# W' of batches 1 to 3 by seven block products instead of eight, with stored sums of w_in's blocks and the softmax's division ahead of its transpose

## The chip, the cores and the metric

The kernel runs on one NeuronCore of a Trainium2 chip. The metric is the device time of one execution in microseconds (us). A profile of one such execution gives for each engine which instruction ran when: PE is the matrix engine, with its weight loads (PEld) listed apart, DVE the vector engine, ACT the scalar engine, POOL (GpSimd) and SP mainly issue transfers (DMA) here.

## The reference: channel attention, then an ELU feed-forward layer

```python
qn = q / (norm(q, axis=1) + 1e-6)            # q, k, v: 4 batches x 6080 tokens x 256 channels
kn = k / (norm(k, axis=1) + 1e-6)
s  = kn.transpose(0, 2, 1) @ qn / tau        # 256 x 256 for each batch
a  = exp(s - max(s)); a /= a.sum(-1) + 1e-9
x  = v @ a                                   # 24320 x 256 over all batches
h  = x @ w_in                                # w_in: 256 x 2048
g  = where(h > 0, h, exp(min(h, 0)) - 1)
out = g @ w_out                              # w_out: 2048 x 256
```

## The kernel before

Per batch the kernel makes one matrix W' = a @ w_in (256 x 2048) and then h = v @ W', so the product v @ a is never made. All matrix products are in fp32r: each operand is split into a high and a low part (ACT casts the high part, DVE subtracts it for the low one), and three matmuls (high by high, high by low, low by high) stand for one product.

The 24320 tokens are 48 chunks of 512 or 496 columns, 12 in a batch. The first four chunks go through a first stage whose order is written by hand, up to about 240 us in the trace. From then on the chunks go in 22 pairs, and h of a pair is made as block products: W' and v are each cut into 2 x 2 blocks, and seven products of sums of blocks (Winograd's form) give what eight products of blocks would. `plan_half` lays down one eighth of a pair: seven products into PSUM banks `bank_a`, `bank_b`, `bank_e` (line 1355; `seed` and `keep` on ACT and `up` and `last` on DVE move partial sums between them), then for four results Relu and Exp on ACT (1383, 1386), the ELU's maximum on DVE (1389), the split of g (ACT 1392, DVE 1395), and the products with w_out into `po` (1413 to 1415).

W' of batch 0 is made in the first stage. For batches 1 to 3 these steps are mixed into the pairs of the batch ahead:

- `plan_rows`: rows of q and k are loaded (SP), split and squared (ACT 1519, 1528; DVE 1531, 1534), and their Gram matrix is summed in the one PSUM bank `pe` (PE 1550, matmuls of 256 columns).
- `plan_soft`: norms, softmax (DVE and ACT, one 128-row half `ct` after the other), `total` (`over_sums`: one over the sums of the softmax), the transposes into `pe` (1676) and the split of the transposed matrix into `aT` (ACT 1683, DVE 1687).
- `plan_s`, once for each quarter `fq` of W' (512 of its 2048 columns): POOL loads the split quarter of w_in, 1 MB, from DRAM (`wi_scr`, line 1429), PE makes two groups of 12 matmuls in all (1451 to 1453, each 128x512, one half of W's rows in a group), both in bank `pe`; ACT copies each group out, times one over the sums (1456). Then four block sums on DVE (836), the high parts by a casting DMA that POOL issues (1471), the low parts on DVE (1478): these are the left factors of the seven products of `plan_half`.

Nothing of this runs in program order. `op(engine, cost, due, fn, deps, takes, uses, lands)` records a step with an assumed cost and a due time; `Ring`s hold the buffers that steps take and give back (`row_ring`: two 8 KB slots for raw rows, v and w_in; `w_ring`: two 4 KB slots; `gram_ring`: the one bank `pe`; `acc_ring` and `square_ring`: one slot each). `best_plan` simulates the five engines, always taking the step that is due first among those that can begin first, shifts due times at random in some stretches of 40 us (`CHANCES` holds the seeds), and the kernel is then written in that order. So each engine works through a fixed list, and an instruction that has to wait holds up all that stands behind it on its engine. `SLACK` stretches the assumed costs, `PACE` spaces the due times.

The core of the step that changes, as it is before:

```python
for jt in range(KT):
    whi, wlo = (in_turns(wi.tile[:, y, jt, :]) for y in range(2))
    nc.tensor.matmul(pw, aT[:, 0, jt, cs], whi, start=(jt == 0), stop=False)
    nc.tensor.matmul(pw, aT[:, 0, jt, cs], wlo, start=False, stop=False)
    nc.tensor.matmul(pw, aT[:, 1, jt, cs], whi, start=False, stop=(jt == KT - 1))
```

Of the kernel before, what the change touches and what calls it, by code (L numbers as in the profile page):

```python
# [57 lines left out]
def channel_attention_then_elu_ffn(ctx: ExitStack, tc, q, k, vT, tau, w_in, w_out, outT):  # L58
# [570 lines left out]
    nc.sync.dma_start(w_scr, wf[0])  # L629
# [280 lines left out]
    SLACK = {ACT: 1.005, DVE: 1.005, POOL: 1.0, PE: 1.003, SP: 1.0}  # L910
# [120 lines left out]
    def best_plan():  # L1031
# [28 lines left out]
    PACE = (10.15, 10.15, 10.15, 10.15)  # L1060
# [275 lines left out]
    DUE = {"products": -20.0, "seed": -20.0, "keep": -19.0, "up": -18.0, "last": -15.0, "terms": -8.0, "soft": -92.0, "soft step": 0.0}  # L1336
# [84 lines left out]

    def plan_s(b, fq, t, deps, state_of):


        wi, xs = Buf(row_ring), [Buf(w_ring) for _ in range(2)]

        def load():
            wi.tile = work.tile([P, 2, KT, CH], F32R, tag="qk", bufs=3, name=f"wi_{fq}")
            nc.gpsimd.dma_start(wi.tile, wi_scr[fq])
# [4 lines left out]
        scaled = []  # L1434
# [4 lines left out]
        else:  # L1439
            got = op(POOL, 0.6, t - 20, load, deps[0:1], [wi], lands=3.8)  # L1440
            got.ready = t - 20
        for ct in range(KT if b else 0):
            bank = Buf(gram_ring)

            def items(ct=ct, bank=bank):
                pw = bank.slot()
                cs = slice(ct * P, ct * P + P)
                aT = state_of["aT"]
                for jt in range(KT):
                    whi, wlo = (in_turns(wi.tile[:, y, jt, :]) for y in range(2))  # L1450
                    nc.tensor.matmul(pw, aT[:, 0, jt, cs], whi, start=(jt == 0), stop=False)
                    nc.tensor.matmul(pw, aT[:, 0, jt, cs], wlo, start=False, stop=False)  # L1452
                    nc.tensor.matmul(pw, aT[:, 1, jt, cs], whi, start=False, stop=(jt == KT - 1))  # L1453

            def scale(ct=ct, bank=bank):
                nc.scalar.activation(
                    x_items(2 * ct, 2 * ct + 2), halves_of_turns(bank.slot()), AF.Copy, scale=state_of["rs"][:, ct : ct + 1]
                )
# [26 lines left out]
    def plan_rows(b, state_of):  # L1485
# [14 lines left out]
        for g in range(begun, NG):  # L1500
            t = t0 + PACE[b - 1] * (1 + over * (g - begun) / (NG - begun))
# [61 lines left out]
    def plan_soft(b):  # L1563
# [105 lines left out]
        total = op(DVE, 0.35, later(), lambda: over_sums(s["rs"]), exps)  # L1669
# [93 lines left out]
```

## Time and profile before

| | |
|---|---|
| median of 3 runs | 2062.77 us (2062.23 to 2062.91) |
| the profiled execution's own time | 2062.74 us |
| its span, first to last instruction | 2061.0 us |
| PE busy | 2053.7 us (100%) |
| ACT busy | 1717.3 us (83%) |
| DVE busy | 1671.0 us (81%) |
| POOL busy | 60.6 us (3%) |
| mean granted clock of PE | 0.999 of full speed |

A matmul's record is longer than the time for which it holds PE, because the next one starts before it ends: the distance between two starts is the price of one in a stream. A record of DVE or ACT likewise ends somewhat after the next one's start can lie. The span leaves out about 1.7 us of the execution's own time.

### The profile page before, as it was taken

Reading aid. Unit: us, or ns where it says so; the run is one execution under the profiler, and the core shown is the slowest. Engines: PE = TensorE matmul, PEld = TensorE weight load, DVE = VectorE, ACT = ScalarE, POOL = GpSimd, SP = SyncE. Lnnn points to the kernel's source line nnn. Section 1 sums busy time; section 2 is a strip of 40 time slices with the busy share of each in tenths; the row PEclk is TensorE's granted clock in tenths of the full one; section 3 lists DMA queues with packets and bytes.
Section 4 is the critical chain, followed back from the end, with each engine's and each line's share of the span. In section 5 each row is a group of like instructions: output and inputs, shape, how many; then the busy total and the mean of one; then the engine's idle time right before and its main releaser. Section 6 shows DMA issues by size and latency. Waiting matters only on the chain.

```text
span 2061.0 us, 28279 instructions
## 1 busy us (share of the span) xinstructions
PE 2053.7 (100%) x9976; PEld 1813.2 (88%) x9976; DVE 1671.0 (81%) x2597; ACT 1717.3 (83%) x3120; POOL 60.6 (3%) x118
## 2 busy tenths in 40 slices
PE   9999999999999999999999999999999999999998
PEld 8888888899888888889888888888888888888887
DVE  7988989888888888887888878878889777677765
ACT  6888789888788988888888888888887788788776
POOL 0000000000100000000000000000001000000000
PEclk9999999999999999999999999999999999999999
DMA  9343332112322121221322212212123110110000
GB/s 357 132 151 99 106 108 82 66 59 96 113 97 82 47 87 57 72 64 46 109 92 89 89 46 75 72 54 84 55 79 135 41 57 16 41 56 16 21 31 20
DMA packets 71806, 164.95 MB, mean 80 GB/s; under 512 B 7536, under 2 KB 16752, under 8 KB 69616
## 3 DMA queue, kind: packets, MB, share of 16 engines
q1 hardware_dynamic: 55968, 118.53, 16.8%
q0 software_dynamic: 15408, 44.11, 6.6%
q8 instruction: 78, 1.28, 0.3%
q14 instruction: 64, 0.52, 0.1%
q10 hardware_dynamic: 288, 0.51, 0.1%
HBM read 100.40 MB, written 31.20 MB: 64 GB/s over the span
## 4 chain that ended last, share of the span: by engine, by line
PE 99%; ACT 0%; DMA 0%; issue 0%; DVE 0%; ACTq 0%; SPq 0%
PE bank_b L1355 16%; PE po L1413 14%; PE po L1414 14%; PE po L1415 14%; PE bank_e L1355 11%; PE bank_a L1355 11%; PE pe L1550 4%; PE gram L497 2%; PE po L423 1%; PE po L422 1%; PE po L421 1%; PE ph L383 1%; PE ph L382 1%; PE ph L381 1%; PE pe L1453 1%; PE pe L1452 1%
## 5 line engine op out<-in xcount | busy, mean ns | idle before, releaser
L1413 PE MATMUL po<-g,wo 128*128 128x512 f32 (+1 forms) x938 | 353.7, 377 | 0.0
L1415 PE MATMUL po<-g,wo 128*128 128x512 f32 (+1 forms) x938 | 353.3, 377 | 0.0
L1414 PE MATMUL po<-g,wo 128*128 128x512 f32 (+1 forms) x938 | 353.2, 377 | 0.0
L1386 ACT ACTIVATE more_e<-more_e 128x512 f32<-128x512 f32 (+1 forms) x562 | 344.2, 632 | 2.5
L1395 DVE TENSOR_TENSOR g<-more_e,g 128x512 fp32r<-128x512 f32 (+1 forms) x371 | 251.2, 681 | 45.4 <-ACT g L1392 43.8
L1392 ACT CAST g<-more_e 128x512 fp32r<-128x512 f32 (+1 forms) x371 | 227.2, 618 | 35.5 <-PE po L1414 18.3
L1389 DVE SCALAR_TENSOR_TENSOR more_e<-more_e,bank_b 128x512 f32<-128x512 f32 (+1 forms) x141 | 96.0, 681 | 141.3 <-ACT more_e L1386 141.3
L1415 PEld LDWEIGHTS po<-g,wo 128*128 128x128 f32 x938 | 177.3, 189 | 22.9
L1413 PEld LDWEIGHTS po<-g,wo 128*128 128x128 f32 x938 | 177.4, 189 | 22.1 <-ACT o_both L1144 0.4
L1414 PEld LDWEIGHTS po<-g,wo 128*128 128x128 f32 x938 | 177.4, 189 | 21.4
L1383 ACT ACTIVATE more_e<-bank_b 128x512 f32<-128x512 f32 (+1 forms) x141 | 83.7, 593 | 128.8 <-PE bank_b L1355 126.4
L1413 PE MATMUL po<-wp,wo 128*128 128x512 f32 (+1 forms) x470 | 177.3, 377 | 0.0
L1415 PE MATMUL po<-wp,wo 128*128 128x512 f32 (+1 forms) x470 | 177.0, 377 | 0.0
L1414 PE MATMUL po<-wp,wo 128*128 128x512 f32 (+1 forms) x470 | 177.0, 377 | 0.0
L1395 DVE TENSOR_TENSOR wp<-more_e,wp 128x512 fp32r<-128x512 f32 (+1 forms) x191 | 130.0, 681 | 22.1 <-ACT wp L1392 21.3
L1355 PE MATMUL bank_a<-term,wp 128*128 128x512 f32 (+1 forms) x528 | 141.5, 377 | 0.0
L1364 DVE TENSOR_TENSOR bank_e<-bank_b,e 128x512 f32<-128x512 f32 (+1 forms) x176 | 121.4, 690 | 22.7 <-ACT e L1362 19.3
L1392 ACT CAST wp<-more_e 128x512 fp32r<-128x512 f32 (+1 forms) x191 | 117.5, 616 | 18.6 <-DVE more_e L1389 9.6
L1368 DVE TENSOR_TENSOR e<-bank_b,e 128x512 f32<-128x512 f32 (+1 forms) x176 | 119.9, 681 | 8.8 <-PE bank_b L1355 8.0
L1550 PEld LDWEIGHTS pe<-rows 128*128 128x128 f32 x804 | 108.7, 191 | 6.2
L1389 DVE SCALAR_TENSOR_TENSOR more_e<-more_e,bank_a 128x512 f32<-128x512 f32 (+1 forms) x141 | 95.4, 676 | 19.8 <-ACT more_e L1386 19.1
L1355 PEld LDWEIGHTS bank_a<-term,wp 128*128 128x128 f32 x528 | 99.3, 189 | 13.0
(325 smaller groups left out, 4755.9 us busy)
## 6 DMA issues: line engine op xcount, KB each, us to landing
v<-in_v_dram SPq DMA_DIRECT2D x13, 1024.0 KB, 4.9
out_dram<-o_both SPq DMA_DIRECT2D x48, 256.0 KB, 2.0
wi<-wi_scr POOLq DMA_DIRECT2D x12, 1024.0 KB, 5.1
w<-in_q_dram SPq DMA_DIRECT2D x34, 256.0 KB, 2.7
w<-in_k_dram SPq DMA_DIRECT2D x34, 256.0 KB, 2.9
v<-in_v_dram SPq DMA_DIRECT2D x8, 992.0 KB, 4.9
more<-in_q_dram SPq DMA_DIRECT2D x30, 256.0 KB, 2.6
more<-in_k_dram SPq DMA_DIRECT2D x30, 256.0 KB, 2.9
```

What stands on the lines that cost most here:

```text
L1355: nc.tensor.matmul(into, ws[x], y, start=(begin and k == 0), stop=(k == 2), skip_group_check=True)
L1364: up = op(DVE, 0.605 * share, t + DUE["up"], lambda: nc.vector.tensor_add(ve, vb, p7.slot[:, 0:n]), [m6, keep], uses=[bank_b, bank_e, p7])
L1368: last = op(DVE, 0.605 * share, t + DUE["last"], lambda: nc.vector.tensor_add(vp(), vb, vp()), [m5, up], uses=[bank_b, p7])
L1383: nc.scalar.activation(ev(), h(), AF.Relu, scale=-1.0)
L1386: nc.scalar.activation(ev(), ev(), AF.Exp, scale=-1.0)
L1389: nc.vector.scalar_tensor_tensor(ev(), ev(), -1.0, h(), op0=ALU.add, op1=ALU.max)
L1392: nc.scalar.copy(g_part(g, 0, n), halves(ev()))
L1395: nc.vector.tensor_sub(g_part(g, 1, n), halves(ev()), g_part(g, 0, n).bitcast(F32))
L1413: nc.tensor.matmul(o, wo[:, f, 0, ds], hi, start=begin, stop=False)
L1414: nc.tensor.matmul(o, wo[:, f, 1, ds], hi, start=False, stop=False)
L1415: nc.tensor.matmul(o, wo[:, f, 0, ds], lo, start=False, stop=end)
L1550: nc.tensor.matmul(pg, r.tile[:, kx, 1, z, cs], in_turns(r.tile[:, qx, 0, z, :]), start=(g == begun and ct == 0 and z == 0 and m == 0), st ...
```

## The change

It touches batches 1 to 3 and the stores that serve them.

- **W' by seven products.** `plan_w` takes the place of the 12 matmuls of 512 columns in `plan_s`: the transposed softmax matrix and each quarter of w_in are cut into 2 x 2 blocks (128 x 128 and 128 x 256), and seven products of 3 matmuls of 256 columns each are made in two takes of bank `pe`. Three partial sums are copied out by ACT (`keep` twice, `c11`), five additions on DVE (`u`, `v`, `c22` and two outputs) finish the four blocks of W'.
- **Sums of w_in's blocks, stored once.** `plan_sums` (in batch 0, once per quarter) loads the exact quarter from `w_scr`, makes the four sums T1 to T4 on DVE, splits them (ACT, DVE) and stores them in `t_scr`. So `w_scr` now holds all four quarters, and `put_by` stores a split quarter of w_in as four blocks. `plan_w` loads a quarter in two takes of `row_ring` (three blocks, then four), four DMAs on POOL, 1.75 MB, where `plan_s` had one of 1 MB.
- **The softmax.** `over_sum` divides its rows by their sums ahead of the transposes, so that W' comes out without a scale. The transposed matrix is kept exact (`a_exact`), DVE makes four block sums of 128 x 128, and eight blocks are split instead of four. The low parts take `square_ring`'s slot, so the next batch's squares wait for it until W' is done.
- **Numbers of the plan.** Assumed costs of ACT and DVE times 1.0075 instead of 1.005, `PACE` 10.22 instead of 10.15, the softmax due 98 us ahead of its batch instead of 92, the rows of q and k spread over 35 paces from pace 2.2 on instead of 36.5, quarters of W' due earlier or later by `W_AT`, other seeds in `CHANCES`.

```diff
+    t_scr = dram.tile([FQ, P, 2, 4, CH // 2], F32, name="t_scr")
+    wi_scr = dram.tile([FQ, 2, 2, P, KT, CH // 2], F32, name="wi_scr")
+    def put_by(fq, parts):
+        for x in range(2):
+            for h in range(2):
+                nc.sync.dma_start(wi_scr[fq, x, h], parts[:, x, :, h * CH // 2 : (h + 1) * CH // 2].bitcast(F32))
...
     def split_wf(fq):
         wis[fq] = work.tile([P, 2, KT, CH], F32R, tag="qk", bufs=3, name=f"wi_0_{fq}")
-        split(wis[fq][:, 0], wis[fq][:, 1], wf.pop(fq))
-        nc.sync.dma_start(wi_scr[fq], wis[fq].bitcast(F32))
+        exact = wf.pop(fq)
+        split(wis[fq][:, 0], wis[fq][:, 1], exact)
+        put_by(fq, wis[fq])
+        nc.sync.dma_start(w_scr[fq], exact)
...
-    SLACK = {ACT: 1.005, DVE: 1.005, POOL: 1.0, PE: 1.003, SP: 1.0}
+    SLACK = {ACT: 1.0075, DVE: 1.0075, POOL: 1.0, PE: 1.003, SP: 1.0}
...
-    PACE = (10.15, 10.15, 10.15, 10.15)
+    PACE = (10.22, 10.22, 10.22, 10.22)
...
+    def plan_sums(fq, t):
+        exact, sums, parts = Buf(w_ring), Buf(w_ring), Buf(row_ring)
...
+        x = op(SP, 0.1, t, lambda: nc.sync.dma_start(exact.slot(), w_scr[fq]), (), [exact], lands=1.9)
+        for y, name in enumerate(("T1", "T3", "T2", "T4")):
+            x = op(DVE, 0.35, t + 8 + y, lambda name=name: total(name, block), [x], [] if y else [sums], [exact, sums] if y else [exact])
+        x = op(ACT, 0.945, t + 14, hi, [x], [parts], [sums])
+        x = op(DVE, 1.145, t + 17, lo, [x], uses=[parts, sums])
+        return op(SP, 0.1, t + 20, lambda: nc.sync.dma_start(t_scr[fq], parts.tile.bitcast(F32)), [x], uses=[parts], lands=3.8)
+
+    def plan_w(fq, t, deps, s, xs, item):
...
+        for k in range(2):
+            for y in sources[k]:
+                due = t - W_LOAD + W_NEXT * k
+                x = op(POOL, 0.6, due, lambda k=k, y=y: load(k, *y), [*deps[0:1], t_done[fq]], [blocks[k]], lands=0.95 * (y[1] - y[0]))
...
+                for n, (i, j) in enumerate(((0, 0), (0, 1), (1, 0))):
+                    nc.tensor.matmul(
+                        at_bank(k, half),
+                        s["aT"][i][:, z],
+                        in_turns(blocks[of].tile[:, j, y]),
...
+        m1 = product(0, 0, "A11", "B11", True, t)
+        p1 = keep(0, 0, 4, t + 1, [m1])
+        m6 = product(0, 1, "S2", "T2", False, t + 0.5, [m1])
+        u = add(lambda: item(5), lambda: at_bank(0, 1), lambda: item(4), t + 2, [m6, p1], banks[0:1])
+        m2 = product(0, 0, "A12", "B21", False, t + 1.5, [p1])
+        c11 = op(ACT, 0.3, t + 3, lambda: nc.scalar.copy(halves(item(0)), halves_of_turns(at_bank(0, 0))), [m2], xs[0:1], banks[0:1])
+        m5 = product(1, 0, "S1", "T1", True, t + 3)
+        m7 = product(1, 1, "S3", "T3", False, t + 3.5, [m5])
+        p7 = keep(1, 1, 6, t + 4, [m7])
...
+        m4 = product(1, 1, "A22", "T4", False, t + 4.5, [p7])
+        m3 = product(1, 0, "S4", "B22", False, t + 5.5, [c22])
...
-            z = op(PE, 1.3, t - 10 + 3 * ct, items, [got, *deps], [bank], [wi, state_of["aT_buf"]], turn=t - 10 + ct)
-            scaled.append(op(ACT, 0.6, t - 8 + 3 * ct, scale, [z], xs[0:1], [bank]))
+            scaled = plan_w(fq, t, deps, state_of, xs, lambda y: x_items(y, y + 1)[:, 0])
...
+        for ct in range(KT):
+            x = op(DVE, 0.25, later(), lambda ct=ct: over_sum(ct), [x])
...
+        x = e = op(ACT, 0.465, later(), a_exact, [pt], (), [turns])
+        for k in range(4):
+            x = op(DVE, 0.21, later(), lambda k=k: a_sum(k), [x])
+        high = op(ACT, 0.51, later(), lambda: a_hi(0), [e, parts, pn], s["aT_bufs"])
```

What stands in a row on PE where batch 2's first quarter of W' is made. The names: `wi` the loaded w_in, `aT` the split softmax matrix (`aT_acc` its high, `aT_sq` its low part), `scr_r` and `wp` left factors, `po` the sums of the output. Before:

```order
L1451 MATMUL pe<-wi_8155,aT_8424 128x512
L1452 MATMUL pe<-wi_8155,aT_8424 128x512
L1453 MATMUL pe<-wi_8155,aT_8424 128x512
L1413 MATMUL po_466<-g_2029,wo 128x496
L1414 MATMUL po_466<-g_2029,wo 128x496
L1415 MATMUL po_466<-g_2029,wo 128x496
L1355 MATMUL bank_b<-terms,scr_r 128x496 x3
```

The same place in the changed kernel, PE:

```order
L1488 MATMUL pe<-wi_0_8313,aT_acc_8572 128x256 x2
L1488 MATMUL pe<-wi_0_8313,aT_sq_8573 128x256
L1362 MATMUL bank_b<-term_1687,scr_r 128x496 x3
L1488 MATMUL pe<-wi_0_8313,aT_acc_8572 128x256 x2
L1488 MATMUL pe<-wi_0_8313,aT_sq_8573 128x256
L1362 MATMUL bank_e<-term_2696,wp_381 128x496 x3
L1362 MATMUL bank_a<-terms_too,wp_381 128x496 x3
L1488 MATMUL pe<-wi_1_8341,aT_acc_8572 128x256 x2
L1488 MATMUL pe<-wi_1_8341,aT_sq_8573 128x256
```

A quarter that was two runs of six full-width matmuls is now seven runs of three half-width ones; between the first product of a bank (m1, just ahead of these rows' first run, m6) and the product that waits for its copy (m2, the second run here) stands one other product of three matmuls.

POOL's list from the first load of batch 2's w_in on, before (`terms` and `term` are v's blocks of a coming pair, `scr_r` and `wp` the left factors):

```order
L1429 DMA wi_8155<-wi_scr 128x2048
L1313 DMA terms<-v_8006 128x496
L1429 DMA wi_8227<-wi_scr 128x2048
L1429 DMA wi_8475<-wi_scr 128x2048
L1471 DMA wp_380<-w_1993 128x768
```

POOL's list at the same place in the changed kernel:

```order
L1467 DMA wi_0_8313<-t_scr 128x2x256
L1467 DMA wi_0_8313<-wi_scr 128x2x512
L1467 DMA wi_1_8341<-wi_scr 128x2x256
L1467 DMA wi_1_8341<-t_scr 128x2x768
L1467 DMA wi_0_8626<-t_scr 128x2x256
L1467 DMA wi_0_8626<-wi_scr 128x2x512
L1467 DMA wi_1_8666<-wi_scr 128x2x256
L1467 DMA wi_1_8666<-t_scr 128x2x768
L1565 DMA scr_r<-w_2009 128x1024
```

Where two quarters of w_in had a slot each, one quarter now fills both slots, and the loads of the next one (`wi_0_8626`) stand behind the last product that reads `wi_0_8313`.

DVE's list around the split of batch 1's transposed softmax matrix, before:

```order
L283 TENSOR_SCALAR sums<-sums 128x2
L284 RECIPROCAL sums<-sums 128x2
L1395 TENSOR_TENSOR g_1966<-more_e,g_1966 128x496
L1364 TENSOR_TENSOR bank_e<-bank_b,e_1886 128x496
L1687 TENSOR_TENSOR aT_4392<-pe,aT_4392 128x512
```

DVE's list there in the changed kernel:

```order
L1766 TENSOR_SCALAR a_671<-a_671,sums 128x256 x2
L1402 TENSOR_TENSOR wp_382<-more_e,wp_382 128x2x248
L1375 TENSOR_TENSOR e_1902<-bank_b,e_1902 128x496
L1396 SCALAR_TENSOR_TENSOR more_e<-more_e,e_1901 128x496
L1792 TENSOR_TENSOR aT_sums_4334<-aT_4333 128x128
L1396 SCALAR_TENSOR_TENSOR e_1903<-e_1903,bank_a 128x496
L1792 TENSOR_TENSOR aT_sums_4334<-aT_sums_4334,aT_4333 128x128
L1803 TENSOR_TENSOR aT_sq_4341<-aT_4333,aT_acc_4340 128x512
```

The division (the first row) now stands ahead of the transposes, and sums of blocks and a second split (further down) come behind them.

## Rows read from the trace of the kernel before

**Rows 1.** The page's head, its busy times by engine, and the first line of the chain of work that ended last (shares of the span).

```profile
span 2061.0 us, 28279 instructions
PE 2053.7 (100%) x9976; PEld 1813.2 (88%) x9976; DVE 1671.0 (81%) x2597; ACT 1717.3 (83%) x3120; POOL 60.6 (3%) x118
...
PE 99%; ACT 0%; DMA 0%; issue 0%; DVE 0%; ACTq 0%; SPq 0%
```

**Rows 2.** The timeline of PE at the four widest openings between two starts behind the first stage: start in us, record's length, line, tiles, form, count; in brackets the idle time that the profile counts.

```profile
241.24 0.38 PE L1415 MATMUL po<-g,wo 128*128 128x512 f32 x1
241.66 0.92 PE L1355 MATMUL bank_e<-term,scr_r 128*128 128x512 f32 x3
...
271.46 0.38 PE L1415 MATMUL po<-g,wo 128*128 128x512 f32 x1
272.19 0.91 PE L1355 MATMUL bank_b<-terms,s_later 128*128 128x512 f32 x3 [0.35 <-ACT bank_b L1360]
272.94 0.81 PE L1355 MATMUL bank_a<-terms,wp 128*128 128x512 f32 x3
...
275.36 0.38 PE L1415 MATMUL po<-g,wo 128*128 128x512 f32 x1
275.70 0.92 PE L1355 MATMUL bank_e<-term,s_later 128*128 128x512 f32 x3
...
284.00 0.38 PE L1415 MATMUL po<-g,wo 128*128 128x512 f32 x1
284.36 0.91 PE L1355 MATMUL bank_b<-terms,s_later 128*128 128x512 f32 x3
```

**Rows 3.** Who waited for whom on PE behind the first stage: us in total, times, longest.

```profile
PE bank_b L1355 <- ACT bank_b L1360: 0.3, 1, 0.3
```

**Rows 4.** The timeline of PE where batch 1's first quarter of W' is made, columns as in rows 2.

```profile
520.03 0.38 PE L1451 MATMUL pe<-wi,aT 128*128 128x512 f32 x1
...
521.11 0.38 PE L1453 MATMUL pe<-wi,aT 128*128 128x512 f32 x1
521.33 0.79 PE L1355 MATMUL bank_e<-term,wp 128*128 128x496 f32 x3
521.96 0.79 PE L1355 MATMUL bank_b<-terms,scr_r 128*128 128x496 f32 x3
...
523.66 0.38 PE L1453 MATMUL pe<-wi,aT 128*128 128x512 f32 x1
```

**Rows 5.** The timeline of PE in a stretch with matmuls of 256 columns beside ones of 512, same columns.

```profile
705.54 0.83 PE L1550 MATMUL pe<-rows 128*128 128x256 f32 x6
706.21 0.81 PE L1355 MATMUL bank_e<-terms,s_later 128*128 128x512 f32 x3
706.86 0.81 PE L1355 MATMUL bank_b<-terms_too,s_later 128*128 128x512 f32 x3
```

**Rows 6.** A group of PE's instructions by line and form over the span, one of three alike (lines 1451, 1452, 1453): count, busy us, mean ns of one record, idle before.

```profile
L1451 PE MATMUL pe<-wi,aT 128*128 128x512 f32 x48 | 18.2, 379 | 0.0
```

**Rows 7.** Groups of DVE's and of ACT's instructions by line and form, from 240 us on: count, busy us, mean ns of one, idle before.

```profile
L1531 DVE TENSOR_TENSOR acc<-acc,sq 128x1024 f32<-128x1024 f32 x65 | 79.5, 1222 | 9.3 <-ACT sq L1528 8.8
...
L1653 DVE TENSOR_SCALAR a<-a,rk 128x256 f32<-128x256 f32 x6 | 2.1, 348 | 0.0
L1687 DVE TENSOR_TENSOR aT<-pe,aT 128x512 fp32r<-128x512 f32 x3 | 2.1, 690 | 0.2 <-ACT aT L1683 0.2
...
L1600 DVE TENSOR_TENSOR a<-pe,a 128x256 f32<-128x256 f32 x2 | 0.7, 416 | 0.0
...
L1631 DVE TENSOR_SCALAR rk<-ry,itau 128x4 f32<-128x4 f32 x3 | 0.7, 219 | 0.0
...
L1519 ACT CAST rows<-w 128x1024 fp32r<-128x1024 f32 x35 | 36.9, 1053 | 1.2 <-DMA w<-in_k_dram 0.5 <-DVE terms_too L1317 0.3 <-PE pe L1550 0.3
...
L1604 ACT COPY a<-pe 128x256 f32<-128x256 f32 x4 | 1.4, 389 | 0.0
```

**Rows 8.** Busy time of each engine (PE, PEld, DVE, ACT, POOL, with counts), granted clock, DMA share and GB/s in four stretches.

```profile
240.00:460.00 220.00, 219.62 (x1111) 193.65 (x1110) 193.07 (x285) 194.70 (x346) 4.75 (x9) 1.00 0.25 84
300.00:350.00 50.00, 50.00 (x253) 44.05 (x252) 46.97 (x68) 47.19 (x85) 1.58 (x3) 1.00 0.30 101
460.00:600.00 140.00, 140.00 (x687) 125.41 (x687) 117.31 (x207) 115.07 (x221) 9.47 (x18) 1.00 0.30 102
...
1450.00:1600.00 150.00, 150.00 (x732) 134.23 (x732) 127.77 (x222) 123.45 (x238) 10.01 (x19) 1.00 0.27 93
```

**Rows 9.** The timeline of ACT at the first copy of W' out of its bank: start, length, and the idle time that the group of rows 4 that ended last had caused.

```profile
521.53 0.69 ACT L1456 ACTIVATE more<-pe,sums 128x512 f32<-128x512 f32 x1 [0.60 <-PE pe L1453]
```

**Rows 10.** POOL's transfers: the issue of w_in's load (line 1429), min/median/max ns; its time from issue to landing, min/median/max us; the same for the casts of the left factors (line 1471); one load in the timeline of POOL.

```profile
L1429 POOL DMA_DIRECT2D wi<-wi_scr x12: 527/527/530, 485.3 to 1567.3; - x12
...
DMA to landing us min/median/max: 4.9/5.1/7.1
...
DMA to landing us min/median/max: 2.8/3.4/7.3
...
524.34 0.53 POOL L1429 DMA_DIRECT2D wi<-wi_scr  x1 [30.19 <-PE pe L1453]
```

**Rows 11.** The timeline of PE in the first stage, matmuls of 256 columns whose operands are plain f32.

```profile
51.82 2.76 PE L497 MATMUL pe<-scr 128*128 128x256 f32 x12
54.41 1.89 PE L324 MATMUL pw<-wf,aT 128*128 128x256 f32 x8
```

More of the change, by code (lines that the diff above doesn't have):

```diff
@@ L1335, in channel_attention_then_elu_ffn @@
     }
-    DUE = {"products": -20.0, "seed": -20.0, "keep": -19.0, "up": -18.0, "last": -15.0, "terms": -8.0, "soft": -92.0, "soft step": 0.0}
+    DUE = {"products": -20.0, "seed": -20.0, "keep": -19.0, "up": -18.0, "last": -15.0, "terms": -8.0, "soft": -98.0, "soft step": 0.0}
     def plan_half(p, fq, j, t, terms, s_done, outs):
@@ L1422, in plan_s, with flat @@
+    def flat(x):
+        return x.rearrange("p a (b t) -> p (a b) t", b=2)
+    A_BLOCKS = ("A11", "A21", "A12", "A22", "S1", "S2", "S3", "S4")
+    SUM_BLOCKS = ("T1", "T3", "T4", "T2")
+    PACKS = (("B11", "B21", "T2"), ("T1", "T3", "T4", "B22"))
+    t_done = {}
     def plan_s(b, fq, t, deps, state_of):
[L1425 to L1429, printed above, removed]
+        xs = [Buf(w_ring) for _ in range(2)]
@@ L1439, in plan_s @@
         else:
[L1440 to L1458, printed above, removed]
-            z = op(PE, 1.3, t - 10 + 3 * ct, items, [got, *deps], [bank], [wi, state_of["aT_buf"]], turn=t - 10 + ct)
-            scaled.append(op(ACT, 0.6, t - 8 + 3 * ct, scale, [z], xs[0:1], [bank]))
+            scaled = plan_w(fq, t, deps, state_of, xs, lambda y: x_items(y, y + 1)[:, 0])
         y = None
@@ L1500, in plan_rows @@
         for g in range(begun, NG):
-            t = t0 + PACE[b - 1] * (1 + over * (g - begun) / (NG - begun))
+            t = t0 + PACE[b - 1] * (ROWS_FROM + over * (g - begun) / (NG - begun))
             n = min(2, RP - 2 * g)
@@ L1676, in transposes @@
                     nc.tensor.transpose(pt[:, jt, ct * P : ct * P + P], s["a"][:, ct, jt * P : jt * P + P], ident)
-        pt = op(PE, 0.4, later(), transposes, exps, [turns], turn=t + 1)
-        s["aT_buf"] = Buf(acc_ring)
-        def aT_hi():
-            s["aT"] = work.tile([P, 2, KT, C], F32R, tag="acc", bufs=1, name=f"aT_{b}")
-            nc.scalar.copy(s["aT"][:, 0], turns.slot().rearrange("p (k c) -> p k c", k=KT))
-        def aT_lo():
-            aT = s["aT"]
-            nc.vector.tensor_sub(aT[:, 1], turns.slot().rearrange("p (k c) -> p k c", k=KT), aT[:, 0].bitcast(F32))
@@ L1689, in plan_soft, with blocks, a_exact @@
-        x = op(ACT, 0.51, later(), aT_hi, [pt, parts], [s["aT_buf"]], [turns])
-        x = op(DVE, 0.605, later(), aT_lo, [x], uses=[turns, s["aT_buf"]])
-        return [last, x, total], s
+        pt = op(PE, 0.4, later(), transposes, [x], [turns], turn=t + 1)
+        s["aT_bufs"] = [Buf(acc_ring), Buf(square_ring)]
+        def blocks(lo, hi):
+            return s["exact"][lo // 4].rearrange("p k (c x) -> p (k c) x", c=2)[:, lo % 4 : lo % 4 + hi - lo]
+        def a_exact():
+            s["exact"] = [work.tile([P, KT, C], F32, tag="a", bufs=1, name=f"aT_{b}")]
+            s["exact"] += [tiny.tile([P, KT, C], F32, tag="early", bufs=1, name=f"aT_sums_{b}")]
+            nc.scalar.copy(s["exact"][0], turns.slot().rearrange("p (k c) -> p k c", k=KT))
@@ new lines, in a_sum, with a_hi @@
+        def a_sum(k):
+            a11, a21, a12, a22, s1, s2, s3, s4 = (blocks(y, y + 1) for y in range(8))
+            to, one, other = ((s1, a21, a22), (s2, s1, a11), (s3, a11, a21), (s4, a12, s2))[k]
+            (nc.vector.tensor_sub if k else nc.vector.tensor_add)(to, one, other)
+        def a_hi(k):
+            if k == 0:
+                s["aT"] = [
+                    work.tile([P, 8, P], F32R, tag=tag, bufs=1, name=f"aT_{tag}_{b}") for tag in ("acc", "sq")
+                ]
+            nc.scalar.copy(s["aT"][0][:, 4 * k : 4 * k + 4], blocks(4 * k, 4 * k + 4))
@@ L1693, in channel_attention_then_elu_ffn @@
+        high = op(ACT, 0.51, later(), lambda: a_hi(1), [x, high], uses=s["aT_bufs"])
+        low = op(DVE, 0.605, later(), lambda: a_lo(1), [high, low], uses=s["aT_bufs"])
+        return [last, low], s
     s_ring = {fq: Ring(fq) for fq in range(FQ)}
@@ L1710, in channel_attention_then_elu_ffn @@
                 s_done[0, fq] = plan_s(0, fq, PACE[0] * (2 * fq - FIRST_S), (), None)
+            for fq in range(FQ):
+                t_done[fq] = plan_sums(fq, SUMS_AT + SUMS_STEP * fq)
         else:
```

96 lines of the change are left out of this document (81 added, 15 removed).

## The prediction

> **What bounds the kernel now.** I began with the head of the page and the chain that ended last [rows 1]: PE is busy for 2053.7 of 2061.0 us, and 99% of the chain is PE. ACT and DVE work for 83% and 81% of the span, but the chain does not pass through them. A busy PE could still hide waits inside overlapping records, so I read the distances between starts next. Behind the first stage the four widest openings [rows 2] are 271.46 to 272.19 us (0.73, where one matmul of 512 columns takes 0.216 [rows 5]: 0.51 lost), 241.24 to 241.66 (0.20 lost), 284.00 to 284.36 (0.14) and 275.36 to 275.70 (0.12). The group of three behind such an opening takes 0.75 (272.19 to 272.94) where 0.65 is usual, 0.1 more each time. Together 1.4 us; and the list of waits on PE has a single line there, 0.3 us [rows 3]. So the time is the length of PE's list. A change gains what it takes out of that list and loses what it makes PE wait, and work on the other engines counts only through such a wait.
>
> **PE's list: the gain.** A quarter of W' is 12 matmuls of 512 columns; six start between 520.03 and 521.33 [rows 4], 0.2158 each with the finer 0.65/3 of [rows 5] beside it (0.2167). With three lines of 48 [rows 6] there are 144: 144 x 0.2158 = 31.07 us. The changed kernel has 12 quarters of 7 x 3 = 21 matmuls of 256 columns, 252. Six of that width take 0.67 us (705.54 to 706.21 [rows 5]), 0.1117 each: half a wide one would be 0.1079, so halving costs 0.004 each. 252 x 0.1117 = 28.14 us. The list gets shorter by **2.9 us**, against the 3.9 us that one product in eight would be without that surcharge. Both forms are fp32r with one weight load each, and weight loads ran beside the matmuls in either. The transposes, Gram matrices and the products of the pairs keep their counts.
>
> The Trainium skill, "TensorE: Matmul & The Clock Gate", section Back-to-back issue gap, gives N/2.4 + 2.5 ns for N columns, that is 109 ns at 256 and 216 at 512, and by that the gain would be 3.6 us; this trace agrees at 512 and not at 256 (112).
>
> **DVE and ACT: more work, under cover.** A quarter adds five additions of 128x256, read from PSUM or SBUF, at 0.416 (line 1600 [rows 7]): 2.1 us, so 8.3 us a batch. The softmax adds two row scalings at 0.348 (line 1653), a second split at 0.690 (line 1687), and four sums of 128x128, a form that the trace lacks: between 0.219 (128x4, line 1631) and 0.416 (128x256), and I take 0.32, half way, as the width is half way too: 0.70 + 0.69 + 1.28 = 2.7 us. So 11.0 us of DVE a batch. From 460 to 600 us DVE works 117.3 of 140 us [rows 8]; 128.3 would be 92%. At batch 3 (1450 to 1600) 127.8 of 150 becomes 138.8, 93%. In batch 0, `plan_sums` adds four times 4 x 0.416 + 1.222 (line 1531's width) = 2.9, 11.6 us in all, to a stretch (240 to 460 us) with 193.1 of 220: 93%. That such shares can be borne is shown by 300 to 350 us: DVE 46.97 and ACT 47.19 of 50 (94%), and PE 50.00. ACT loses two copies of 0.69 [rows 9] a quarter and gains three of 0.389 (line 1604), 0.2 less; the sums' casts add four times 1.05 (line 1519) once. I take nothing for either engine; the bound above is a rival below.
>
> **New waits inside W'.** Products m2 and m4 reuse a half bank that ACT has just copied. A copy began 0.42 us after the last matmul of its group had begun (521.11 [rows 4] to 521.53 [rows 9]) and takes 0.389, so m2 may start 0.81 us behind m1's last start. At the tightest place (batch 2's first quarter) m6 and one product of 496 columns stand between: 0.11 + 0.34 + 0.63 (521.33 to 521.96 [rows 4]) = 1.08 us. That holds if ACT is free; behind a step like the 0.69 of [rows 9] it is late by up to 0.4. Twice in 12 quarters that is 0 to 10 us; nearest is the same shape in the pairs, `seed` behind m1, 176 times in this run with 0.3 us of wait in all [rows 3]. I take 0.
>
> **POOL: the reload.** Four loads a quarter for one: 36 more issues of 0.53 us [rows 10], on an engine 3% busy. Queued behind them on POOL are the casts of v's blocks and of the left factors, whose order the plan has moved with them. But the cover shrinks. Before, each quarter had one slot: the third was loaded at 524.34, when the first was through, and the second, already there, lay between. Now a quarter fills both slots of `row_ring`, and the next quarter's first take is loaded only when the last product of the present first take is through. In PE's new list 24 matmuls of 496 columns (0.209) and 12 of 256 stand between these two: 5.02 + 1.34 = **6.4 us**, at five places (7.0 at a sixth); elsewhere it is over 10 us. What has to fit: a load was issued 0.68 us after the start of the matmul that freed its slot (523.66 [rows 4] to 524.34 [rows 10]), 0.47 behind that matmul's place; the second issue 0.53 later; landing, for pairs of 512 and 384 KB issued in this way, 2.8 to 7.3 us, median 3.4 (line 1471 in [rows 10]; now it is 512 and 256 KB). Together 4.4 us, with 2.0 to spare; at the maximum 8.3, 1.9 late. I take 0 and keep six times 0 to 1.9 for the range.
>
> A rule of the Trainium skill speaks against these loads: "SBUF — State Buffer", section SBUF: two separate sides, says that a DMA issued from POOL has its descriptors written through a port that VectorE can hold for a whole instruction, so that the transfer starves meanwhile. Estimated from one DVE step of 0.69 us ahead of each of two issues that is 1.4 us, 5.8 in place of 4.4, still below 6.4; no row shows it, as all 12 issues took 527 to 530 ns with DVE at 84%.
>
> **SP and the softmax's chain.** SP gets 23 more issues in the whole run; the blocks' stores stand ahead of q and k rows that are squared four steps later, and SP mostly waits. Nothing. The longer softmax chain (2.7 us of DVE, a copy and a cast on ACT) is due 6 us earlier, and after W' its left factors are still read some 40 us later in PE's list, as before. Nothing.
>
> **The sum.** The profiled execution took 2062.74 us, the median of the runs is 2062.77; from the latter 2062.77 - 2.93 = **2059.8 us**, 0.14% less. What a measurement of this kernel can tell from no change is about 0.2%, 4.1 us: faster ends at 2058.6, slower begins at 2066.9.
>
> **The rivals.**
> 1. *The openings close too.* The order behind 236 us is planned anew with slower assumed engines, and 1.4 us of openings [rows 2] could go: 2059.8 - 1.4 = 2058.4, just over the line to faster. For it: they lie at the start of the planned part. Against: DVE gets more work exactly there.
> 2. *Some reloads come late.* Two of six at the maximum landing: 2059.8 + 3.8 = 2063.6. For it: 2.0 us to spare and landings up to 7.3. Against: the median.
> 3. *DVE becomes the bound in batch 0 (slower).* The 11.6 us of `plan_sums` fall into 240 to 460 us. If they land where DVE is full, each of them delays splits that PE needs: 2059.8 + 11.6 = 2071.4. It decides where DVE's demand passes the stretch: 193.1 + 11.6 leaves 15 of 220 us; an added 7.1 us of wait is needed to be slower by over 0.2%. All six reloads late (2059.8 + 11.4 = 2071.2) is the same side by another door.
> 4. *A narrow matmul costs more than half.* From 31.07/252 = 0.123 us on, the list gets longer. The f32 ones of the same width took 0.216 (51.82 to 54.41, 12 of them [rows 11]); at that price 252 x 0.216 = 54.4, 23 us more: 2086. Then the change would not do what it says. Against: its tiles are fp32r as in the 0.1117 of [rows 5]. The same section of the skill gives sustained spacings of about 131 ns at 512 and 81 at 128, by which narrowing is a loss as well; the trace has 216 at 512 and contradicts it.
>
> **How the numbers follow.** Forecast 0.64, rival 1 0.14, rival 2 0.10, rival 3 with its second door 0.10, rival 4 0.02. Faster is rival 1, 0.14; same the forecast and rival 2, 0.74; slower rivals 3 and 4, 0.12. For 8 in 10 the range leaves out rivals 3 and 4 (0.12) and half of rival 1 (0.07): from 2058.2 to 2064.0, which holds two late reloads, or 4 of the 10 us of waits inside W'.
>
> **What would show it.** Right: a group of three matmuls of W' takes 0.335 us from start to start; PE's openings sum to about what they did; DVE at 91 to 94% in the stretches named and PE at 100% there. Wrong: lines in PE's waits that name `pe` and a load of `wi` (rival 2), or ACT's or DVE's copies and sums of `pe` (the chain in W'); openings between 290 and 460 us behind DVE (rival 3); the narrow matmuls at another spacing (rival 4).

## The result, and the profile after

The changed kernel takes **2073.31 us** (median of 4 runs, 2072.46 to 2074.42) against 2062.5 of the kernel before beside it: 10.8 us more, ratio 1.0051, 95% interval 1.0039 to 1.0063. The forecast of 2059.8 and its whole range (2058.2 to 2064.0) were wrong; by the prediction's own bound of 0.2% this is slower, an outcome to which it gave 0.12. The profiled execution took 2072.46 us, its span is 2070.7.

Head of the page, busy time by engine and the chain by engine, as in [rows 1]:

```profile
span 2070.7 us, 28454 instructions
...
PE 2055.9 (99%) x10084; PEld 1811.0 (87%) x10084; DVE 1704.9 (82%) x2698; ACT 1727.9 (83%) x3142; POOL 88.7 (4%) x154
...
PE 95%; DVE 2%; ACT 1%; DMA 1%; issue 0%; SPq 0%; POOL 0%; ACTq 0%; DVEq 0%
```

PE's part of the chain was 99%; now DVE and ACT stand in it. PE's waits (in all, times, longest), which had a single line behind the first stage [rows 3]:

```profile
PE bank_b L1362 <- ACT bank_b L1367: 3.1, 2, 2.5
PE pe L1488 <- DVE more L1504: 1.4, 5, 0.4
...
PE pe L1644 <- DVE rows L1628: 0.9, 1, 0.9
PE bank_e L1362 <- DVE more_e L1396: 0.7, 3, 0.3
PE bank_b L1362 <- DVE bank_e L1371: 0.5, 1, 0.5
PE pe L1488 <- DMA wi<-wi_scr: 0.4, 2, 0.2
```

Line 1488 is a product of W', 1362 a product of a pair, 1644 the Gram matrix. The windows of [rows 8] again (PE, PEld, DVE, ACT, POOL, clock, DMA share, GB/s):

```profile
240.00:460.00 220.00, 217.76 (x1105) 191.52 (x1104) 198.45 (x297) 193.92 (x337) 4.74 (x9) 1.00 0.34 112
300.00:350.00 50.00, 48.39 (x243) 41.65 (x242) 46.22 (x68) 45.33 (x80) 1.57 (x3) 1.00 0.39 132
460.00:600.00 140.00, 137.15 (x702) 122.25 (x701) 121.85 (x227) 114.75 (x228) 17.73 (x28) 1.00 0.37 113
1450.00:1600.00 150.00, 148.75 (x756) 132.45 (x755) 123.75 (x223) 119.64 (x231) 16.28 (x26) 1.00 0.30 92
```

PE stood for 2.2, 1.6, 2.9 and 1.3 us in them, and in the second and the fourth it waits although DVE and ACT are both *less* busy than before (DVE 46.97 and 127.77, ACT 47.19 and 123.45).

For a full account I took the distance of every two starts on PE behind 235 us, less the median distance for that pair of widths, and added up the differences over 15 ns. I call these **openings** (a slower matmul behind a stand is counted with them):

| kernel | median us | openings us | of it at products of W' |
|---|---|---|---|
| before | 2062.5 | 6.3 | 0 |
| changed | 2073.3 | 19.6 | 5.6 |

Openings grew by 13.3 us. PE's last matmul ended at 2055.27 us before and at 2065.57 after, so the list without openings went from 2049.0 to 2046.0: 3.1 us shorter. Of these, 0.2 us belong to the first stage, which came to its first product of a pair at 229.57 us instead of 229.80; the planned part is 2.8 us shorter. 13.3 - 3.1 = 10.2 us, against 10.3 between the two ends. Three places hold most of it: products of W' (5.6 us, at 13 places), batch 0 from 250 to 332 us (4.4, where the kernel before has 1.5 by the same count from 235 to 335), and a single opening at 501 us (2.65).

A place in W' (timeline of the changed kernel: start, length, engine, line; the shown instructions only):

```profile
561.87 0.37 ACT L1501 COPY w<-pe 128x256 f32<-128x256 f32 x1
...
562.63 0.37 PE L1422 MATMUL po<-g,wo 128*128 128x496 f32 x1
562.67 0.42 DVE L1504 TENSOR_TENSOR w<-pe,w 128x256 f32<-128x256 f32 x1
...
563.14 0.30 PEld L1488 LDWEIGHTS pe<-wi,aT_acc 128*128 128x128 f32 x2 [0.52 <-DVE w L1504]
563.14 0.49 PE L1488 MATMUL pe<-wi,aT_acc 128*128 128x256 f32 x2
```

The product at 563.14 is m2. It writes the half of `pe` that ACT had copied out from 561.87 to 562.24; yet it starts 0.05 us after DVE has read the *other* half (the sum `u`, 562.67 to 563.09). PE's list of this program says the same. These are the rows of the first quarter of batch 1 (m1, m6 and m2, first matmul of each), with the waits that the program holds:

```
1916 L1488 MATMUL pe<-wi_0_4120,aT_acc_4340 128x256 [waits DMASW1_49]
1919 L1488 MATMUL pe<-wi_0_4120,aT_acc_4340 128x256 [waits DMASW0_49,Activation_49]
1926 L1488 MATMUL pe<-wi_0_4120,aT_acc_4340 128x256 [waits DVE_49]
```

m6 waits for ACT (the copy p1 of m1's half) and m2 for DVE (u), though `plan_w` gives the planner m1 alone for m6 and p1 alone for m2. The Trainium skill, "PSUM — Partial Sum Buffer", section PSUM bank collisions raise a hardware error, states a rule that such a wait follows: accesses of two engines are to be guarded by bank, not by address. The trace agrees (m2 starts 0.05 us behind the end of u), and the prediction did not weigh it.

### The profile page after: what moved, and what is told of

Its sections match the earlier page's. It is cut to its first block, busy times and chain, and to the rows that moved or that the text cites. A ratio compares the mean times of both kernels' runs of the same rounds, so it can differ in the third digit from the quotient of the medians.

```text
span 2070.7 us, 28454 instructions
## 1 busy us (share of the span) xinstructions
PE 2055.9 (99%) x10084; PEld 1811.0 (87%) x10084; DVE 1704.9 (82%) x2698; ACT 1727.9 (83%) x3142; POOL 88.7 (4%) x154
## 3 DMA queue, kind: packets, MB, share of 16 engines
q1 hardware_dynamic: 61328, 126.39, 17.9%
## 4 chain that ended last, share of the span: by engine, by line
PE 95%; DVE 2%; ACT 1%; DMA 1%; issue 0%; SPq 0%; POOL 0%; ACTq 0%; DVEq 0%
PE bank_b L1362 16%; PE po L1420 14%; PE po L1422 14%; PE po L1421 14%; PE bank_e L1362 11%; PE bank_a L1362 11%; PE pe L1644 4%; PE gram L503 2%; PE pe L1488 1%; PE po L429 1%; PE po L427 1%; PE po L428 1%; PE ph L387 1%; PE ph L389 1%; PE ph L388 1%; DMA wi<-wi_scr 1%
## 5 line engine op out<-in xcount | busy, mean ns | idle before, releaser
L1362 PE MATMUL bank_e<-term,wp 128*128 128x512 f32 (+1 forms) x528 | 141.5, 377 | 0.0
L1362 PE MATMUL bank_a<-term,wp 128*128 128x512 f32 (+1 forms) x432 | 115.7, 377 | 0.0
L1644 PE MATMUL pe<-rows 128*128 128x256 f32 x804 | 110.7, 275 | 0.9 <-DVE rows L1628 0.9
```

The costliest lines, as they stand in the source:

```text
L1362: nc.tensor.matmul(into, ws[x], y, start=(begin and k == 0), stop=(k == 2), skip_group_check=True)
L1644: nc.tensor.matmul(pg, r.tile[:, kx, 1, z, cs], in_turns(r.tile[:, qx, 0, z, :]), start=(g == begun and ct == 0 and z == 0 and m == 0), st ...
```

## The experiments

**Theory 1:** the waits between the halves of `pe`, unknown to the planner, make the openings of W'. **Theory 2:** the DVE work of `plan_sums` makes those of batch 0 (the prediction's rival 3). **Theory 3:** the order that comes out of the new numbers makes what lies outside W', whatever the amount of work. The rivals stand with each run. The kernel before, run beside these kernels each time, took 2062.4 to 2063.2 us.

### u_off and readers_off: no DVE read of the other half

```diff
-u = add(..., lambda: at_bank(0, 1), lambda: item(4), ...)
+u = add(..., lambda: item(4), lambda: item(4), ...)
 # readers_off, besides:
-c22 = add(..., lambda: halves_of_turns(at_bank(1, 0)), lambda: halves_of_turns(item(7)), ...)
+c22 = add(..., lambda: halves_of_turns(item(7)), lambda: halves_of_turns(item(7)), ...)
```

> The changed kernel with one DVE step altered: u, the sum of the copied product m1 and of m6, no longer reads m6 from bank pe (it adds the copy to itself, so W' is not the reference's). Orders, instruction counts and durations stay. Theory 1 (halves of one bank): m2, which needs only the half that ACT copied out, in fact waits until DVE has read the other half. Then the openings of the changed kernel that end with a DVE sum of pe (those before 563.14, 587.71, 1073.01, 1100.13, 1580.88 and 1593.16 us) vanish, 2.0 us with the slower group behind each, and the time is about 2071.3. Rival (the prediction's own term: ACT's copy p1 comes late): m2 still waits for the copy, the openings stay within 0.1 us each and the time stays at 2073.3.

> As the run before, and c22 too reads no bank (W' is not the reference's). Theory 1 (halves of one bank, with DVE's sums as the late step): the openings at 1029.55, 1053.66, 1536.87, 1561.88 and 1585.04 go as well, 2.7 us, and with them the two that follow 2 to 3 us later at 1032.5 and 1539.9 (0.9): with the 2.0 of u some 5.6 us in all, about 2067.7. Of the openings ahead of products of W' only the one at 575.35 stays, which ends with a load. Rival (ACT's copies p1 and p7 come late): the openings move by under 0.1 us each, and the time stays within 1 us of 2073.3. Second rival (a wait only goes to the next step): the openings go but others of the same size stand behind them in the pairs, and the time falls by less than half of 5.6 us.

Measured: u_off 2073.42 us (2070.82 to 2074.95), span 2069.0, openings 17.9, at W' 4.3. readers_off 2070.63 (2068.66 to 2070.73), span 2068.9, openings 17.5, at W' 2.2. The same place in u_off (timeline of PE):

```profile
562.68 0.37 PE L1422 MATMUL po<-g,wo 128*128 128x496 f32 x1
562.89 0.38 PE L1488 MATMUL pe<-wi,aT_acc 128*128 128x256 f32 x2
563.11 0.28 PE L1488 MATMUL pe<-wi,aT_sq 128*128 128x256 f32 x1
563.22 0.79 PE L1362 MATMUL bank_e<-terms_too,s_later 128*128 128x496 f32 x3
```

No opening, and the three matmuls take 0.33 us. Five of the six openings named for u are gone (the sixth, 0.1 us, became 0.2), and in readers_off the five named for c22; the lines of products of W' behind DVE left PE's waits (one of those five keeps 0.1 us). ACT's copies were not what was late at these places. (m3 needs c22's read in any case, so not all of readers_off's gain comes from hidden waits.) The sizes were too high: the openings at 1032 and 1539 us stayed (0.34 each), so they are not knock-ons of W', and waits for loads of `wi` took some back (0.65 us at 576, where it was 0.39). Both times missed what was expected (2071.3 and 2067.7). The median of u_off did not move; the span of its profile fell by 1.7 us, but its runs spread over 4 us. The median of readers_off fell by 2.7 us, just under half of 5.6, which was the second rival's sign; yet no openings of that size stand behind the old places (from 1000 to 1100 us they sum to 1.2 instead of 2.4, from 1500 to 1620 to 1.6 instead of 3.7). One reason for the spread and for the small fall shows in the profile of readers_off. Its windows around the opening at 501 us (PE, PEld, DVE, ACT, POOL, clock, DMA share, GB/s):

```profile
501.50:504.40 2.90, 0.43 (x3) 0.04 (x1) 2.28 (x6) 2.90 (x8) 0.00 (x0) 1.00 0.45 175
504.40:507.50 3.10, 3.08 (x8) 2.55 (x9) 2.30 (x7) 2.44 (x6) 0.00 (x0) 0.53 0.25 97
```

Behind the standing PE the granted clock fell to about half, the lower level of 1.2 GHz, and eight distances were 0.2 us longer: 1.6 us more. In the changed kernel's profile the same opening left the clock at 1.00:

```profile
501.20:504.00 2.80, 0.34 (x2) 0.00 (x0) 2.17 (x6) 2.80 (x8) 0.00 (x0) 1.00 0.46 176
504.00:507.00 3.00, 2.96 (x14) 2.71 (x15) 2.37 (x8) 3.00 (x8) 0.00 (x0) 1.00 0.22 85
```

Without these 1.6 us readers_off had 15.9 us of openings, 3.7 below the changed kernel; its lowest run lies 3.8 below the changed kernel's lowest.

### sums_off: batch 0 without the added DVE work

```diff
-x = op(DVE, 0.35, t + 8 + y, lambda name=name: total(name, block), ...)
+x = op(DVE, 0.35, t + 8 + y, lambda: None, ...)
 # hi() casts the exact quarter instead of the sums, and the store writes that high part twice (two DMAs)
 def lo():
-    nc.vector.tensor_sub(parts.tile[:, 1], flat(sums.slot()), parts.tile[:, 0].bitcast(F32))
+    pass
```

> The changed kernel without the DVE work of plan_sums: the four sums of a quarter and their low part are not made (20 DVE instructions less in all, about 11.6 us; what is stored is a copy of the exact quarter, so W' of batches 1 to 3 is not the reference's). The order of everything else stays. Theory 2 (the prediction's rival 3: DVE is full in batch 0, and what plan_sums adds makes PE wait): the openings from 250 to 332 us, 4.2 us with the slower groups behind them, shrink to the 1.4 us or so of the kernel before, and the time is about 2070. Rival (the new order, not the added work, makes these openings): they stay at 4 us, and the time at 2073.3. The opening of 2.65 us at 501 us stays in both cases, since no sum is made there.

Measured: 2073.29 us (2071.95 to 2074.35), openings 19.1. Theory 2 fell: the openings of batch 0 are the same, to 0.02 us. The widest, in the timelines of PE of the changed kernel and of sums_off:

```profile
319.44 0.27 PE L1644 MATMUL pe<-rows 128*128 128x256 f32 x1
320.62 1.05 PE L1644 MATMUL pe<-rows 128*128 128x256 f32 x7 [0.91 <-DVE rows L1628]
```

```profile
319.73 0.27 PE L1648 MATMUL pe<-rows 128*128 128x256 f32 x1
320.88 0.82 PE L1648 MATMUL pe<-rows 128*128 128x256 f32 x5 [0.89 <-DVE rows L1632]
```

The low part of the rows still comes at the same place of DVE's list, behind steps that wait for ACT. The run tests less of the amount than the 11.6 us suggest: from 250 to 332 us, where these openings lie, DVE's busy time fell only from 72.49 to 70.22 us, one quarter's share, and the opening before 251.77 lies ahead of all that work. The other three quarters' work lies behind 332 us, and from there to 460 us PE does not stand in the changed kernel either (busy 128.00 of 128.00 us). So the added work of `plan_sums` is not the cause; that the place in the list is, is read from the timeline here.

### softmax_thin: the opening at 501 us

```diff
-nc.vector.reciprocal(s["ry"][:, w], s[of][:, w])
+nc.vector.tensor_scalar(s["ry"][:, w], s[of][:, w], 1.0, None, op0=ALU.mult)
-x = op(DVE, 0.25, later(), lambda ct=ct: over_sum(ct), [x])
+x = op(DVE, 0.25, later(), lambda: None, [x])
```

> The changed kernel with the order kept and DVE's part of the softmax made lighter: the four reciprocals of 128x130 (0.96 us each) are multiplications by one (some 0.22), and the two row scalings that the change adds are left out, so the result is not the reference's; 3.6 us of DVE less per batch. Theory 3 (the order makes the opening of 2.65 us at 501 us: in PE's list a single product stands between the last product of a bank and the one that needs Relu, Exp, the maximum and the seed behind it): the opening stays between 2.2 and 2.9 us, and the time within 1.5 us of 2073.3. Rival (DVE, dense with the softmax's work, is late there): the opening falls to 1.5 us or less, and the time with it to about 2071.

Measured: 2074.16 us (2072.11 to 2075.26). The opening is the same: 2.86 us from the third start of `bank_a` at 501.40 to 504.26, 2.65 more than the usual 0.21 (PE's timeline):

```profile
500.98 0.79 PE L1362 MATMUL bank_a<-terms_too,wp 128*128 128x496 f32 x3
504.26 0.89 PE L1362 MATMUL bank_b<-term,scr_r 128*128 128x496 f32 x3 [2.49 <-ACT bank_b L1367]
```

So DVE's load is not it either. In the changed kernel the chain there is this (timeline; Exp, the maximum that frees `bank_b`, the softmax's Exp, the seed, and the product):

```profile
501.90 1.12 ACT L1393 ACTIVATE more_e<-more_e 128x496 f32<-128x496 f32 x2
502.55 0.67 DVE L1396 SCALAR_TENSOR_TENSOR more_e<-more_e,bank_b 128x496 f32<-128x496 f32 x1 [0.60 <-ACT more_e L1393]
502.91 0.51 ACT L1754 ACTIVATE a<-a,nm 128x256 f32<-128x256 f32 x1
...
503.40 0.58 ACT L1367 COPY bank_b<-bank_a 128x496 f32<-128x496 f32 x1
...
504.04 0.48 PE L1362 MATMUL bank_b<-term,scr_r 128*128 128x496 f32 x1 [2.49 <-ACT bank_b L1367]
```

DVE even stands idle for 0.60 us in it. PE's list has one product between the last use of `bank_b` and the next one; elsewhere more work stands there. ACT, though, is busy through the whole opening (2.80 of 2.80 us in the windows above), and no run thins ACT's part; that the list makes this opening is read from the trace, not tested by itself.

### before_numbers and after_oldnumbers: work and numbers crossed

```diff
 # before_numbers, in the kernel before (after_oldnumbers: the reverse in the changed one, W_AT 0)
-SLACK = {ACT: 1.005, DVE: 1.005, ...}; PACE = (10.15, ...); "soft": -92.0
+SLACK = {ACT: 1.0075, DVE: 1.0075, ...}; PACE = (10.22, ...); "soft": -98.0
-ROWS_OVER = 36.5; FIRST_OVER = 22; FIRST_S = 3
+ROWS_OVER = 35 (from pace 2.2); FIRST_OVER = 19.5; FIRST_S = 4.5; CHANCES of the change
```

> The kernel before with the change's plan numbers alone (SLACK 1.0075, PACE 10.22, the softmax due 98 us ahead, ROWS_OVER 35 from pace 2.2, FIRST_OVER, FIRST_S and the seeds in CHANCES): no work is added or taken out, only the order is planned anew. Theory 3 (the numbers cost something by themselves): openings of several us in all turn up at places of its own, among them near 501 us, where the changed kernel has 2.65 us and no added work but the softmax's, and the time is 2066 to 2070. Rival (numbers are neutral, what costs is the added work and the waits inside W'): openings stay below 2.5 us in all and the time is within 2 us of the kernel before, 2062.5.

> The work of the change with the numbers and seeds of the kernel before (the fourth corner beside the kernel before, the changed kernel and the kernel before with the change's numbers, which took 7.9 us longer). Theory 3 (numbers and seeds fit one amount of work only): openings turn up in many places, in batch 3 too, where no W' is made for a next batch, and the time is 2080 or more, far above both 2070.3 and 2073.3. Rival (the change's numbers are simply worse, by the same 8 us in either kernel): the time is 2073.3 - 7.9 = 2065.4 or less.

| median us (openings us) | numbers of before | numbers of the change |
|---|---|---|
| work of before | 2062.4 (6.3) | 2070.25 (14.7) |
| work of the change | 2096.5 (44.2) | 2073.3 (19.6) |

Both as theory 3 had it, the first 0.25 us above the expected 2066 to 2070. (In after_oldnumbers, steps that only the change has keep its other numbers.) Without a single added instruction the kernel before loses 7.9 us, 1.7 us of openings from 500 to 550 us among it. PE's waits in that run:

```profile
PE bank_e L1354 <- DVE more_e L1388: 2.2, 4, 1.0
PE po L1412 <- ACT o_both L1143: 1.2, 2, 1.0
...
PE bank_e L1354 <- DVE e L1388: 0.9, 2, 0.4
```

And with the old numbers the changed work is 34 us slower than the kernel before, with openings in batch 3, where no W' is made (PE's timeline of after_oldnumbers):

```profile
1936.27 0.38 PE L1423 MATMUL po<-g,wo 128*128 128x512 f32 x1
1937.96 0.48 PE L1421 MATMUL po<-g,wo 128*128 128x496 f32 x1 [1.32 <-ACT o_both L1152]
```

In these two kernels numbers and seeds fit one amount of work only; the time of the diff as a whole does not tell them apart from the work. The two runs also do not tell the numbers from the seeds, which were changed together.

### deps_s, replanned and replanned_blind: the planner told the waits

```diff
-p1 = keep(0, 0, 4, t + 1, [m1])
 m6 = product(0, 1, "S2", "T2", False, t + 0.5, [m1])
+p1 = keep(0, 0, 4, t + 1, [m6])
-m2 = product(..., [p1])
+m2 = product(..., [u])
-m4 = product(..., [p7])
-m3 = product(..., [c22])
+m4 = product(..., [c22])
+m3 = product(..., [m4])
 # replanned, besides: other due times in plan_w, SLACK 1.005, PACE 10.28, "soft" -103, FIRST_OVER 20.5, FIRST_S 4, ...
 # replanned_blind: the numbers of replanned, plan_w as in the change
```

> The changed kernel in which plan_w tells the planner the waits that its steps really have inside bank pe (m6 directly behind m1 and ahead of the copy p1, m2 behind the sum u, m4 behind c22, m3 behind m4, both outputs behind m3), all other numbers of the change kept, with new seeds in CHANCES, since the old ones belong to another list. Nothing is left out. Theory 1 (halves of one bank): PE's list now has other work where these waits lie, so openings ahead of products of W' sum to under 1.5 us (6.4 in the changed kernel, 4.4 without those that turned out not to belong to W'), those of batch 0 and near 501 us may stay, as the numbers are kept: 2066 to 2070. Rival (the waits only move: the chain of copies and sums is longer than what PE has to put between): lines of pe behind DVE or ACT still sum to over 3 us in PE's waits, and the time stays above 2071.

> The same true waits and, besides, other numbers of the plan throughout (SLACK 1.005, PACE 10.28, softmax 103 us ahead, rows from pace 1.2, FIRST_OVER 20.5, FIRST_S 4, sums at 50 and then every 55 us, W_AT -8, -2, -12, 2, W_LOAD 11, new seeds). All the work of the change is in it. Theory 3 (the planned order, not the amount of work, makes the openings of batch 0 and at 501 us): with an order that suits the work the openings behind 235 us sum to 6 to 8 us as in the kernel before (6.3), and what is left is the shorter list, 3.1 us: 2060 to 2062. Rival (DVE's and ACT's added work fills the stretches of the softmax and of batch 0, whatever the order): openings there stay at 5 us or more above the kernel before's, and the time is 2064 or more.

> The numbers of the replanned kernel (SLACK 1.005, PACE 10.28, softmax 103 us ahead and so on) with plan_w as the change has it, so that the planner again doesn't know of the waits inside bank pe; seeds of its own. Nothing is left out. Theory 1 (halves of one bank, unknown to the planner): openings ahead of products of W' come back, 3 us or more with the slower matmuls behind them (5.6 in the changed kernel, 0.5 in the replanned one), each ended by DVE or ACT reading pe; with what the other order leaves elsewhere 2068 to 2074. Rival (the better numbers alone remove them, since DVE and ACT then come in time): under 1.5 us ahead of products of W', and the time is 2063 to 2067.

| kernel | median us (range) | openings us | at W' |
|---|---|---|---|
| deps_s | 2071.39 (2070.64 to 2072.22) | 18.6 | 3.5 |
| replanned | 2063.43 (2062.74 to 2063.93) | 9.6 | 0.5 |
| replanned_blind | 2075.35 (2074.11 to 2077.03) | 23.0 | 8.1 |

deps_s came out at its rival's time, though PE's waits for DVE ahead of products of W' sum to 2.2 us and not to over 3: under the change's numbers, telling the planner was not enough, and a chain that is now seen in full still found too little work to stand in it (one opening of 1.9 us at 586). With other numbers as well, the whole work of the change takes what the kernel before takes (ratio 1.0002, 0.9993 to 1.0011). That lies between the two expectations: not 2060 to 2062 with 6 to 8 us of openings, and not 2064 or more. The engines' busy times, PE's waits, and the window of batch 0 there:

```profile
PE 2054.2 (100%) x10084; PEld 1814.0 (88%) x10084; DVE 1705.1 (83%) x2698; ACT 1725.7 (84%) x3142; POOL 88.6 (4%) x154
```

```profile
PE pd L200 <- DVE ones L112: 1.1, 1, 1.1
PE pn L225 <- DVE acc L222: 0.4, 1, 0.4
PE bank_b L1362 <- DVE bank_e L1371: 0.4, 1, 0.4
```

```profile
240.00:460.00 220.00, 219.55 (x1115) 194.18 (x1114) 199.93 (x299) 199.11 (x349) 4.74 (x9) 1.00 0.33 109
```

DVE is as busy as in the changed kernel and ACT within 2.2 us of it, and from 240 to 460 us both are busier than there while PE stands for only 0.5 us; so the added work does not force openings. Take the telling away again and the waits of W' come back in PE's list (replanned_blind, 1.4 us above the expected 2074 at most; 1.6 us of its 23.0 are half clock behind an opening of 2.1 us at 498):

```profile
PE pe L1488 <- DVE more L1504: 1.4, 4, 0.6
...
PE pe L1488 <- DVE w L1504: 0.6, 2, 0.3
...
PE pe L1488 <- ACT w L1501: 0.3, 1, 0.3
```

Openings outside W' came back too, which the telling alone does not explain. Outside W' the four kernels with all of the change's work have (at W' in brackets):

| openings us | planner not told | planner told |
|---|---|---|
| numbers of the change | 14.0 (5.6) | 15.0 (3.5) |
| numbers of replanned | 14.9 (8.1) | 9.1 (0.5) |

So neither the telling nor the other numbers closed the openings outside W' by itself. Each kernel has seeds of its own, one set each, and the shares of telling, numbers and seeds outside W' are not separated.

## Why the prediction was wrong

- **PE's list, -2.9 us: right.** Without openings the planned part of the list is 2.8 us shorter, and a group of three takes 0.33 us as forecast.
- **"New waits inside W' ... I take 0": the step that failed first.** It asked only for ACT's copies, of the same half. The waits that decide are for DVE's reads of the other half, which the planner was not told of. The openings at W' sum to 5.6 us (0.46 of it at a load), inside the 0 to 10 that was worked out, of which the range held only 4; on their own they would have brought the time to 2065.4, outside the range. The comparison with `seed` in the pairs did not hold: there a product fills its bank, and the planner is told each wait.
- **"DVE and ACT ... I take nothing", "SP and the softmax's chain. Nothing", and rival 1: the second and larger failure.** Each judged the added work by the room that the engines have, and took it that a newly planned order would be as tight as the old one. Openings outside W' went from 6.3 to 14.0 us, 7.8 us more. Taking added work out at fixed order left them (sums_off, softmax_thin); other numbers and seeds at fixed work made as many (before_numbers); and with another order the same work has 9.1 (replanned). Rival 1 had them close by 1.4. The evidence that an order is only as good as its numbers was in the diff, as changed seeds and paces, and got no price.
- **Rival 3, 2071.4 us: near the time by luck, wrong in mechanism.** DVE did not become the bound: the work of `plan_sums` could be taken out without effect. DVE's share was 82 to 90% in the three stretches for which 92 to 93% was forecast. The sum of the added DVE work was too large as well: 3 x 11.0 + 11.6 = 44.6 us of whole records, though records overlap; the busy time grew by 33.9.
- **Reloads, 0 to 1.9 us at six places: the value 0 was nearly right.** PE's matmuls waited 0.4 us in all for loads of `wi`, one opening of 0.46 us with what follows it at 575. The median landing was 4.2 us, longer than the 3.4 assumed, but at most 6.5, though each issue too took longer than assumed (below).
- **Rivals 2 and 4** did not happen.

What stays open: which of the changed numbers or seeds spoils which stretch was not separated. Nor does any kernel here turn the shorter list into time. In replanned the planned part without openings is 2.9 us shorter than before, but it has 9.6 us of openings where the kernel before has 6.3, most of them under 0.15 us each, and in its profile the first stage came to its first product of a pair 0.7 us later (230.52 us against 229.80).

## What to carry to other kernels

Where a fixed order feeds the bounding engine, price a new order apart from the new work: cross the two (old work with new numbers, new work with old ones, each with more than one set of seeds) before reading the result as the worth of an algorithm. Here two products in one PSUM bank shared their waits: give the planner the waits that the program really holds, and read them from its list, not from the code's data flow. To tell "too much work" from "wrong place", thin the suspected work at unchanged order.

## What the runs showed of the hardware

- A PE that stood for 2.49 us by the list of waits lost its clock in one profile and not in another: in readers_off 0.53 was granted for 3.1 us behind the opening, in the changed kernel 1.00. Such an opening costs 2.65 or 4.3 us; that this is what spreads the runs of these kernels is likely, but only one execution of each was profiled.
- POOL took 0.70 to 0.72 us to issue a load of `wi` in pieces, of 256 KB or of 768 KB alike; the one whole load of before took 0.53 [rows 10]. Rows of POOL in the changed kernel (ns, shortest, median, longest):

```profile
L1467 POOL DMA_DIRECT2D wi<-t_scr x24: 698/710/720, 484.2 to 1601.1; - x24
...
DMA to landing us min/median/max: 2.9/4.2/6.5
```
